# The gradient of z in a linear-attention backward pass: from extra matmul columns to GpSimd and VectorE

## The chip, the cores and the metric

One core of a Trainium2 chip runs the whole kernel. The metric is the device time in microseconds; the kernel before has a median of 641.99 us over six runs (641.56 to 644.08).

## The reference, cut to what matters

The forward pass is a gate over two branches: linear attention with 32 heads of 20 columns, and a two-layer ReLU network. All gradients are asked for as well.

```python
g = _sigmoid((x * gate_w).sum(-1, keepdims=True))
# attention: phi(t) = where(t > 0, t + 1, exp(t)) + 1e-6
pq, pk = phi(q), phi(k)
kv  = einsum("bhsd,bhse->bhde", pk, v)
z   = einsum("bhsd->bhd", pk)                      # sum over the tokens
num = einsum("bhqd,bhde->bhqe", pq, kv)
den = einsum("bhqd,bhd->bhq", pq, z)[..., None] + 1e-6
a   = (num / den) @ wo
b   = relu(x @ w1) @ w2
out = g * a + (1 - g) * b
```

There are 2048 tokens (16 tiles of 128 rows), D = 640 (5 tiles of 128 columns) and 1728 hidden columns. The gradient of z is one number for each of the 640 columns: a sum over all tokens of pq / den times a number for each token and head, with a minus sign. It is wanted in every row of the gradient of k.

## The kernel before

The work is a row of TensorE stages, one after the other: k and the gate, Y = pk^T x, the forward loop over the token tiles (q, the hidden layer, the output), dW2, X, the backward loop over the token tiles (`fb_a` and `fb_b`), dW1, dk, dWk, dWq and dx. A scheduler orders the instructions of every engine by their dependences and their place in the program; each engine then runs its own queue in order. SyncE issues nearly all loads, stores and transposing loads. Large buffers lie in one SBUF tensor, the arena, whose addresses a planner assigns from sizes and rough times of life (`ar.add`, lines 107 to 177), so that buffers of different stages share addresses and a later writer waits for an earlier reader.

The parts that the change and the prediction speak of:

- `pqg(i)` is pq / den times the gate for token tile i (bf16, 128 rows, 640 columns). `doX(i)` holds dO of the tile, loaded by `do_load`, and 32 more columns (`DX = D + H`, line 108). In the forward loop (lines 637 to 655) `do_load` of the next group of four tiles stands at the head of an iteration.
- `r_main(i)`, run for every token tile during the dW2 stage, multiplies dO by M^T, and reduces its product with pqg over each head into `u_all[:, i, :]` (32 columns, f32, line 672). `w32` is `u_all` times `rg_t` (one number for each token, line 674). GpSimd multiplies `zb` by it (line 676), and ScalarE puts it, as bf16, in the 32 extra columns of `doX(i)` (line 677).
- At the end of dW2, GpSimd adds the two halves of its last tile (line 737), after a DMA has moved one half to other partitions. Then VectorE computes `U_t` and `dl_t` (lines 744 to 746).
- X = pqg^T [dO, w32] runs over five tiles of 128 columns of pqg, and for each over the 16 token tiles, as two matmuls of 512 and 160 columns (lines 755 and 756). The first 640 columns are X. Of the last 32, the block diagonal is what is wanted: VectorE multiplies them by the mask `MDh` and sums (line 759) to give -dz, one column of `dz_t`, and spreads it on a diagonal, `dzd` (line 761). In `small_1` a matmul with a matrix of ones sums the rows of `dzd` and so puts dz in all 128 rows (`dzb`).
- `fb_a(i, half)` (lines 766 to 783): ten matmuls of 432 columns fill a PSUM tile, ScalarE scales it into a buffer of the ring `tb` (line 775; eight buffers), VectorE makes a mask from the hidden layer in another one (line 777) and multiplies (line 778); after the second half it copies 64 columns (line 780) and SyncE issues a transposing load. `fb_b` uses that four tiles later.
- `small_0`, after `fb_a` of tile 2, fills five PSUM tiles `dwo`, which ScalarE and VectorE evacuate in turns (lines 344 and 346). `small_1`, after tile 5, starts with a GpSimd memset (line 807), which the scheduler may run as soon as its addresses are free.
- PSUM has four buffers of this size, used in turns by all stages. The SBUF tag `f32` has three.

Of the kernel before, what the change touches and what calls it, by code (L numbers as in the profile page):

```python
# [8 lines left out]
ALU = mybir.AluOpType  # L9
# [71 lines left out]
def kernel(  # L81
# [23 lines left out]
    WMAX = max(hi - lo for lo, hi in WIN)  # L105
    DSPL = [(0, 512), (512, D)]
    DSP1 = [(0, 512), (512, D + 1)]
    DX = D + H
    DQX = D + 16

    ar = _Arena()
# [21 lines left out]
    ar.add("pk", NT * D * B2, 0, T_FF)  # L133
    ar.add("zd", D * B2, 0, T_FF - 5)
    ar.add("YT0", KD * D * B2, T_Y, T_FF + 5)
    ar.add("dzd", D * B2, T_X, T_FB + 50)
    ar.add("warm", 512 * B2, 0, 10)
    ar.add("Y", KD * D * B2, T_Y, T_FF + 20)
    ar.add("KVT", KD * D * B2, 0, T_FF + 30)
# [53 lines left out]
    def aview(name, n_elems, **dims):  # L193
        o = ar.off(name) // 2
        v = arena[:, o:o + n_elems]
        if dims:
            (k, n), = dims.items()
            v = v.rearrange(f"p ({k} z) -> p {k} z", **{k: n})
        return v
# [24 lines left out]
    doTg = [aview(f"doT{g}", G * D, k=KD) for g in range(NG)]  # L224
    hsg = [aview(f"hs{g}", G * FPAD, i=G) for g in range(NG)]
    zd, YT0_s = aview("zd", D), mat("YT0")
    dzd = aview("dzd", D)
    wk_s, wq_s, wv_s, wo_s = aview("wk", KD * DQX, k=KD), mat("wq"), mat("wv"), mat("wo")
    w1_s = aview("w1", KD * F, k=KD)
    w2_s = aview("w2", KF * D, k=KF)  # L230
# [21 lines left out]
    def pqg(i):  # L252
        return pqgg[i // G][:, i % G, :]

    def doX(i):
        return doXg[i // G][:, i % G, :]
# [24 lines left out]
    ones_sq = cpool.tile([P, P], BF16, name="ones_sq")  # L281
    zc_t = cpool.tile([P, KD], FP32, name="zc_t")
    MDw = cpool.tile([P, KD, WMAX], BF16, name="MDw")
    MDh = cpool.tile([P, KD, H], BF16, name="MDh")
    zb = cpool.tile([P, D], BF16, name="zb")
    dzb = cpool.tile([P, D], BF16, name="dzb")
    dz_t = cpool.tile([P, KD], FP32, name="dz_t")
    w1T_tail = cpool.tile([P, D], BF16, name="w1T_tail")
    rg_t = cpool.tile([P, NT], FP32, name="rg_t")
    g_t = cpool.tile([P, NT], FP32, name="g_t")  # L290
# [35 lines left out]
    def after(late, early, wait=False):  # L326
        tc.add_manual_dep(late.ins, early.ins.name, mybir.DependencyInfo(
            mybir.DependencyClass.Sync if wait else mybir.DependencyClass.NoSync,
            mybir.DependencyReason.DATA), reason="order of loads")
# [141 lines left out]
    for i in range(NT):  # L471
        if i >= NPE:
            k_part(i, range(KD))
        if i == 0:
            nc.vector.memset(ones_sq[:], 1.0)
            nc.gpsimd.memset(MDw[:], 1.0)
            nc.gpsimd.memset(MDh[:], 1.0)

    for j in range(KD):
        rel = P * j - WIN[j][0]  # L480
        nc.gpsimd.affine_select(out=MDw[:, j, :], in_=MDw[:, j, :], compare_op=ALU.is_ge, fill=0.0,
                                base=rel, pattern=[[-DH, WMAX // DH], [0, DH]], channel_multiplier=1)
        nc.gpsimd.affine_select(out=MDw[:, j, :], in_=MDw[:, j, :], compare_op=ALU.is_ge, fill=0.0,
                                base=DH - 1 - rel, pattern=[[DH, WMAX // DH], [0, DH]], channel_multiplier=-1)
        nc.gpsimd.affine_select(out=MDh[:, j, :], in_=MDh[:, j, :], compare_op=ALU.is_ge, fill=0.0,
                                base=P * j, pattern=[[-DH, H]], channel_multiplier=1)
        nc.gpsimd.affine_select(out=MDh[:, j, :], in_=MDh[:, j, :], compare_op=ALU.is_ge, fill=0.0,
                                base=DH - 1 - P * j, pattern=[[DH, H]], channel_multiplier=-1)
    nc.gpsimd.memset(KVT_s, 0.0)
    nc.vector.tensor_scalar(rg_t[:], rg_t[:], 1.0, None, ALU.add)  # L490
    nc.vector.reciprocal(g_t[:], rg_t[:])
# [45 lines left out]
    def h_half(i, half):  # L537
        hp = pp("hp")
        for nb in range(2):
            blk = 2 * half + nb  # L540
            for k in range(KD):
                nc.tensor.matmul(hp[:, nb, 0:NBW], lhsT=xT(i, k), rhs=w1_s[:, k, blk * NBW:(blk + 1) * NBW],  # L542
                                 start=(k == 0), stop=(k == KD - 1))
        dst = hs(i)[:, 2 * half * NBW:(2 * half + 2) * NBW].rearrange("p (b c) -> p b c", b=2)
        if half == 0:
            nc.scalar.activation(dst, hp[:, :, 0:NBW], ACT.Relu, scale=omg_t[:, i:i + 1])
        else:
            nc.vector.tensor_scalar(dst, hp[:, :, 0:NBW], omg_t[:, i:i + 1], 0.0, ALU.mult, ALU.max)
            nc.vector.tensor_copy(hs(i)[:, F:FPAD], hs(i)[:, F - FT:F])
            hTs[i] = rnext("hTf").rearrange("p (c s) -> p c s", s=P)  # L550
            hT_ld[0] = load_T(hTs[i], hs(i))
# [8 lines left out]
    def out_chunk(i):  # L560
        pr, ii = i // 2, i % 2
        hT, pqT = hTs.pop(i), pqTs.pop(i)
        if ii == 0:
            ops[i] = pp("op")
        op = ops.pop(i)
        for kf in range(KF - 1):
            mm_cols(op, hT[:, kf, :], lambda a, e: w2_s[:, kf, a:e], ii == 0 and kf == 0, False)
        for k in range(KD):
            mm_cols(op, pqT[:, k, :], lambda a, e: M_s[:, a // P:e // P, k, :], False, ii == 1 and k == KD - 1)
        if ii == 0:  # L570
            ops[i + 1] = pp("op")
            tail_pair(op, ops[i + 1], hT[:, KF - 1, :], hTs[i + 1][:, KF - 1, :], w2_s[:, KF - 1, :], True)
        if ii == 0:
            o_st[pr] = rnext("ost").rearrange("p (i d) -> p i d", i=2)
        nc.scalar.copy(o_st[pr][:, ii, :], flat(op)[:, 0:D])
        jk = tmp("tb", 8)
        nc.vector.scalar_tensor_tensor(jk[:], flat(op)[:, 0:D], 1.0, doX(i)[:, 0:D], ALU.mult, ALU.mult,
                                       accum_out=T_t[:, i:i + 1])
        if ii == 1:
            nc.scalar.dma_start(rows2(o0, pr), o_st.pop(pr))  # L580

    def do_load(g):
        return load_N(doXg[g][:, :, 0:D], do2[g * G * P:(g + 1) * G * P, :])
# [52 lines left out]
    LAG = 2  # L636
    for a in range(2, NT + LAG, 2):
        if a < NT:
            if a % G == 2 and a // G + 1 < NG:
                after(do_load(a // G + 1), M_ld)  # L640
            if a > 2:
                q_main(a)
                q_den(a)
                h_half(a, 0)
            q_post(a)
            h_half(a, 1)
            q_main(a + 1)
            q_den(a + 1)
            h_half(a + 1, 0)
            q_post(a + 1)  # L650
        q_store(a // 2 - 1)
        out_chunk(a - 2)
        if a < NT:
            h_half(a + 1, 1)
        out_chunk(a - 1)
    e_r, dq_st = {}, {}

# [6 lines left out]
    def r_main(i):  # L664
        rp = pp("rp")
        for k in range(KD):
            mm_cols(rp, doTg[i // G][:, k, gsl(i)], lambda a, e: MT_s[:, k, a:e], k == 0, k == KD - 1)
        rb = tmp("tb", 8)
        nc.scalar.copy(rb[:], flat(rp)[:, 0:D])
        t_ = tmp("tb", 8)  # L670
        nc.vector.tensor_tensor(t_[:], rb[:], pqg(i), ALU.mult)
        nc.vector.tensor_reduce(u_all[:, i, :], heads(t_[:]), AX.X, ALU.add)
        w32 = tmp("grd", 3, [P, H], FP32)
        nc.vector.tensor_scalar(w32[:], u_all[:, i, :], rg_t[:, i:i + 1], None, ALU.mult)
        wz = tmp("f32", 3, dt=FP32)
        nc.gpsimd.tensor_tensor(heads(wz[:]), heads(zb[:]), hb(w32[:]), ALU.mult)
        nc.scalar.copy(doX(i)[:, D:DX], w32[:])
        rps[i] = rp, wz

    def r_post(i):  # L680
# [61 lines left out]
                after(ld, last_mm)  # L742
    r_store(NT // 2 - 1)
    nc.vector.tensor_reduce(U_t[:], u_all[:], AX.X, ALU.add)
    nc.vector.tensor_tensor(dl_t[:], g_t[:], T_t[:], ALU.mult)
    nc.vector.tensor_tensor(dl_t[:], U_t[:], dl_t[:], ALU.subtract)

    for q_ in range(2):
        load_T(w1T_s[:, 0:KF - 1, q_ * 320:(q_ + 1) * 320], B_w1[q_ * 320:(q_ + 1) * 320, 0:(KF - 1) * P])
    nc.gpsimd.tensor_copy(w1T_s[:, KF - 1, :], w1T_tail[:, :])  # L750
    for m in range(KD):
        xp = pp("xp")
        for i in range(NT):
            lhsT = pqg(i)[:, csl(m)]
            nc.tensor.matmul(xp[:, 0, :], lhsT=lhsT, rhs=doX(i)[:, 0:512], start=(i == 0), stop=(i == NT - 1))  # L755
            nc.tensor.matmul(xp[:, 1, 0:DX - 512], lhsT=lhsT, rhs=doX(i)[:, 512:DX], start=(i == 0), stop=(i == NT - 1))  # L756
        nc.scalar.copy(X_s[:, m, :], flat(xp)[:, 0:D])
        jz = tmp("grd", 3, [P, H], FP32)
        nc.vector.scalar_tensor_tensor(jz[:], flat(xp)[:, D:DX], -1.0, MDh[:, m, :], ALU.mult, ALU.mult,
                                       accum_out=dz_t[:, m:m + 1])  # L760
        nc.vector.tensor_scalar(dzd[:, csl(m)], ident[:], dz_t[:, m:m + 1], None, ALU.mult)
    load_T(KV2_s, KVT_d)

    dhTs, dx_st = {}, {}
# [41 lines left out]
    def small_1():  # L806
        nc.gpsimd.memset(dKVT_s, 0.0)  # L807
        ps = pp("dzp")
        mm_cols(ps, ones_sq[:], lambda a, e: dzd[:, a:e], True, True)
        nc.scalar.copy(dzb[:], flat(ps)[:, 0:D])  # L810
        blockdiag(dKVT_s, woT_s, XT_s)

# [201 lines left out]
```

## Time and profile before

| What | us |
|---|---|
| median of six runs | 641.99 |
| the profiled execution, its time | 641.73 |
| its span, first to last instruction | 640.0 |
| VectorE busy | 240.8 |
| ScalarE busy | 151.3 |
| GpSimd busy | 98.7 |
| dW2 stage, X stage start | 217.6, 298.2 |
| backward loop start (first `fb_a` matmul) | 321.0 |

The granted TensorE clock is 1.000 in the mean over the span. A row of the order of time has the start and the duration in us, the engine, the line, the operation, output<-inputs, and in brackets the idle time of the engine before it with what ended it. Rows of one operation on a line give the duration in ns as minimum/median/maximum, and then the first and last start. "PE" is TensorE, "DVE" VectorE, "ACT" ScalarE, "POOL" GpSimd, "SP" SyncE.

### The profile page before, as it was taken

How to read it: one execution, taken by the hardware profiler on the slowest of the kernel's cores; microseconds unless marked ns; L12 is line 12 of the kernel's file. 1: busy time of each engine (PE TensorE's matmuls, PEld its weight loads, DVE VectorE, ACT ScalarE, POOL GpSimd, SP SyncE). 2: the span in 40 equal slices, each digit the busy share in tenths (PEclk: the TensorE clock that was granted, in tenths of full speed). 3: DMA queues.
4: the chain of work that ended last, by engine and by line, in shares of the span. 5: the costliest groups of instructions: out<-in, count | busy, mean ns of one | idle time of the engine just before them, and what ended most of it. 6: DMA issues, size and time to landing. Idle time of an engine off the chain costs nothing.

```text
span 640.0 us, 10518 instructions
## 1 busy us (share of the span) xinstructions
PE 635.0 (99%) x4462; PEld 354.5 (55%) x4462; DVE 240.8 (38%) x494; ACT 151.3 (24%) x223; POOL 98.7 (15%) x97
## 2 busy tenths in 40 slices
PE   8999999999999999999999999999999999999998
PEld 4556555555555555555555555555555555555554
DVE  4822754454534146554153332230016320104442
ACT  3512321222211123322153343431100011110000
POOL 5002642454334022322000000000000000000000
PEclk9999999999999999999999999999999999999999
DMA  7998995434355943942869997992228559991111
GB/s 183 344 391 173 254 236 131 120 92 82 87 120 102 268 122 102 193 143 85 188 152 240 256 225 154 195 261 64 89 76 174 139 143 238 244 248 42 42 42 43
DMA packets 227075, 103.69 MB, mean 162 GB/s; under 512 B 183764, under 2 KB 226324, under 8 KB 227028
## 3 DMA queue, kind: packets, MB, share of 16 engines
q1 hardware_dynamic: 216602, 90.23, 61.2%
q10 hardware_dynamic: 10426, 12.78, 5.8%
q8 instruction: 35, 0.57, 0.4%
q14 instruction: 12, 0.10, 0.0%
HBM read 28.43 MB, written 28.84 MB: 89 GB/s over the span
## 4 chain that ended last, share of the span: by engine, by line
PE 98%; ACT 1%; DVE 0%; issue 0%
PE w1p_4596 L857 1%; PE w1p_4727 L857 1%; PE w1p_5115 L857 1%; PE w1p_5047 L857 1%; PE w1p_4824 L857 1%; PE w1p_5240 L857 1%; PE w1p_5183 L857 1%; PE w1p_4978 L857 1%; PE w1p_4659 L857 1%; PE w1p_4528 L857 1%; PE op_2274 L339 1%; PE op_2237 L339 1%; PE op_2137 L339 1%; PE op_1786 L339 1%; PE op_1591 L339 1%; PE op_1554 L339 1%
## 5 line engine op out<-in xcount | busy, mean ns | idle before, releaser
L339 PEld LDWEIGHTS <-arena 128*128 128x128 bf16 x2818 | 218.2, 98 | 169.7 <-DVE arena L346 1.0
L857 PEld LDWEIGHTS <-arena 128*128 128x128 bf16 x320 | 30.8, 98 | 26.9 <-issue 0.5
L771 PEld LDWEIGHTS <-arena 128*128 128x128 bf16 x320 | 30.5, 98 | 26.7 <-issue 1.3
L542 PEld LDWEIGHTS <-arena 128*128 128x128 bf16 x320 | 30.0, 98 | 26.6 <-issue 1.9
L841 DVE TENSOR_TENSOR tb_4802<-dkp_4791,dzb 128x640 bf16<-128x640 f32 x1 | 0.8, 825 | 41.5 <-PE dkp_4791 L339 41.5
L755 PEld LDWEIGHTS <-arena 128*128 128x128 bf16 x80 | 7.8, 98 | 9.5 <-issue 0.3
L944 PEld LDWEIGHTS <-arena 128*128 128x128 bf16 x80 | 7.8, 98 | 9.5
L956 DVE SCALAR_TENSOR_TENSOR f_5645<-gwb,dl_t,arena 128x640 f32<-128x640 bf16 x1 | 0.9, 883 | 26.4 <-DMA arena<-dxB_d 26.4
L361 PEld LDWEIGHTS <-arena 128*128 128x128 bf16 x140 | 7.9, 97 | 1.9 <-issue 0.6
L508 POOL TENSOR_TENSOR f_728<-tb_492,zb 128x640 f32<-128x640 bf16 x1 | 1.4, 1397 | 48.1 <-ACT zb L605 48.1
L756 PEld LDWEIGHTS <-arena 128*128 128x128 bf16 x80 | 7.8, 98 | 0.0
L945 PEld LDWEIGHTS <-arena 128*128 128x128 bf16 x80 | 7.8, 98 | 0.0
L807 POOL MEMSET arena<- 128x3200 bf16 x1 | 2.8, 2764 | 30.5 <-ACT arena L344 30.5
L857 PE MATMUL w1p_4596<-arena 128*128 128x432 bf16 x32 | 6.0, 346 | 0.0
L857 PE MATMUL w1p_4727<-arena 128*128 128x432 bf16 x32 | 6.0, 346 | 0.0
L857 PE MATMUL w1p_4528<-arena 128*128 128x432 bf16 x32 | 6.0, 346 | 0.0
L857 PE MATMUL w1p_4824<-arena 128*128 128x432 bf16 x32 | 6.0, 346 | 0.0
L857 PE MATMUL w1p_5047<-arena 128*128 128x432 bf16 x32 | 6.0, 346 | 0.0
L857 PE MATMUL w1p_5115<-arena 128*128 128x432 bf16 x32 | 6.0, 346 | 0.0
L857 PE MATMUL w1p_4659<-arena 128*128 128x432 bf16 x32 | 6.0, 346 | 0.0
L857 PE MATMUL w1p_4978<-arena 128*128 128x432 bf16 x32 | 6.0, 346 | 0.0
L857 PE MATMUL w1p_5183<-arena 128*128 128x432 bf16 x32 | 6.0, 346 | 0.0
(1048 smaller groups left out, 1189.1 us busy)
## 6 DMA issues: line engine op xcount, KB each, us to landing
out_dram<-arena ACTq DMA_DIRECT2D x28, 160.0 KB, 3.4
arena<-in_A_x_dram SPq DMA_DIRECT2D x6, 640.0 KB, 6.2
pk_d<-arena SPq DMA_DIRECT2D x4, 640.0 KB, 9.4
arena<-in_grad_out_dram SPq DMA_DIRECT2D x4, 640.0 KB, 5.1
e_d<-arena SPq DMA_DIRECT2D x8, 320.0 KB, 2.4
out_dram<-arena ACTq DMA_DIRECT2D x8, 320.0 KB, 2.3
arena<-e_d SPq DMA_DIRECT2D x8, 320.0 KB, 3.8
dq_d<-arena SPq DMA_DIRECT2D x8, 320.0 KB, 4.0
```

Source lines behind the costliest of these rows:

```text
L339: mm = nc.tensor.matmul(ps_tile[:, b, 0:e - a], lhsT=lhsT, rhs=rhs_fn(a, e), start=start, stop=stop, **kw)
L361: nc.tensor.matmul(ps_tile[:, bank, a - 512 * bank:e - 512 * bank], lhsT=lhsT_fn(j), rhs=rhs_mat[:, j, a:e], start=bank not in seen, stop= ...
L508: return nc.gpsimd.tensor_tensor(tzs[i][:], pqs[i][:], zb[:], ALU.mult)
L542: nc.tensor.matmul(hp[:, nb, 0:NBW], lhsT=xT(i, k), rhs=w1_s[:, k, blk * NBW:(blk + 1) * NBW], start=(k == 0), stop=(k == KD - 1))
L755: nc.tensor.matmul(xp[:, 0, :], lhsT=lhsT, rhs=doX(i)[:, 0:512], start=(i == 0), stop=(i == NT - 1))
L756: nc.tensor.matmul(xp[:, 1, 0:DX - 512], lhsT=lhsT, rhs=doX(i)[:, 512:DX], start=(i == 0), stop=(i == NT - 1))
L771: nc.tensor.matmul(gp[:, nb, 0:NBW], lhsT=doTg[i // G][:, k, gsl(i)], rhs=w2T_s[:, k, blk * NBW:(blk + 1) * NBW], start=(k == 0), stop=(k ...
L807: nc.gpsimd.memset(dKVT_s, 0.0)
L857: nc.tensor.matmul(wp[:, nb, 0:NBW], lhsT=xN2[:, i, csl(m)], rhs=hs(i)[:, blk * NBW:(blk + 1) * NBW], start=(i == 0), stop=(i == NT - 1))
L944: nc.tensor.matmul(wp[:, 0, :], lhsT=lhsT, rhs=dqN[:, i, 0:512], start=(i == 0), stop=(i == NT - 1))
L945: nc.tensor.matmul(wp[:, 1, 0:D + 1 - 512], lhsT=lhsT, rhs=dqN[:, i, 512:D + 1], start=(i == 0), stop=(i == NT - 1))
L956: nc.vector.scalar_tensor_tensor(base[:], gwb[:], dl_t[:, i:i + 1], dxB[:, i, :], ALU.mult, ALU.add)
```

## The change

The 32 extra columns of X go, and with them the cast into `doX`, the mask `MDh`, `dz_t` and the diagonal `dzd`. In their place `u_all` is multiplied by `rg_t` once for all tiles. While X runs, GpSimd multiplies `pqg(i)` by `u_all[:, i, :]`, one number for each head of 20 columns, for all 16 token tiles, three or four beside each tile of X, and VectorE adds the 16 products in f32 into `dz_a`, a buffer of the tag `f32`. A last VectorE operation changes the sign and makes bf16 of it, `dzs`: 128 rows of partial sums. The matmul with ones in `small_1`, which sums rows anyway, takes `dzs` in place of the diagonal. The arena's `doX` buffers get smaller, which gives the planner other addresses. Besides, `do_load` of the next group moves to the end of the iteration, between `h_half(a + 1, 1)` and `out_chunk(a - 1)`.

```diff
-    DX = D + H
+    DX = D
...
-    ar.add("dzd", D * B2, T_X, T_FB + 50)
+    ar.add("dzs", D * B2, T_X, T_FB + 50)
...
-    MDh = cpool.tile([P, KD, H], BF16, name="MDh")
...
-            nc.gpsimd.memset(MDh[:], 1.0)
...
-        nc.gpsimd.affine_select(out=MDh[:, j, :], in_=MDh[:, j, :], compare_op=ALU.is_ge, fill=0.0,
-                                base=P * j, pattern=[[-DH, H]], channel_multiplier=1)
...
     for a in range(2, NT + LAG, 2):
         if a < NT:
-            if a % G == 2 and a // G + 1 < NG:
-                after(do_load(a // G + 1), M_ld)
...
             h_half(a + 1, 1)
+            if a % G == 2 and a // G + 1 < NG:
+                after(do_load(a // G + 1), M_ld)
         out_chunk(a - 1)
...
         nc.gpsimd.tensor_tensor(heads(wz[:]), heads(zb[:]), hb(w32[:]), ALU.mult)
-        nc.scalar.copy(doX(i)[:, D:DX], w32[:])
...
     nc.vector.tensor_reduce(U_t[:], u_all[:], AX.X, ALU.add)
+    nc.vector.tensor_tensor(u_all[:], u_all[:], rg_t[:].unsqueeze(2).to_broadcast([P, NT, H]), ALU.mult)
...
+    dz_a = tmp("f32", 3, dt=FP32)
     for m in range(KD):
         xp = pp("xp")
         for i in range(NT):
-            lhsT = pqg(i)[:, csl(m)]
-            nc.tensor.matmul(xp[:, 0, :], lhsT=lhsT, rhs=doX(i)[:, 0:512], start=(i == 0), stop=(i == NT - 1))
-            nc.tensor.matmul(xp[:, 1, 0:DX - 512], lhsT=lhsT, rhs=doX(i)[:, 512:DX], start=(i == 0), stop=(i == NT - 1))
+            mm_cols(xp, pqg(i)[:, csl(m)], lambda a, e: doX(i)[:, a:e], i == 0, i == NT - 1)
         nc.scalar.copy(X_s[:, m, :], flat(xp)[:, 0:D])
-        jz = tmp("grd", 3, [P, H], FP32)
-        nc.vector.scalar_tensor_tensor(jz[:], flat(xp)[:, D:DX], -1.0, MDh[:, m, :], ALU.mult, ALU.mult,
-                                       accum_out=dz_t[:, m:m + 1])
-        nc.vector.tensor_scalar(dzd[:, csl(m)], ident[:], dz_t[:, m:m + 1], None, ALU.mult)
+        for i in range(NT * m // KD, NT * (m + 1) // KD):
+            pr_ = dz_a if i == 0 else tmp("f32", 3, dt=FP32)
+            nc.gpsimd.tensor_tensor(heads(pr_[:]), heads(pqg(i)), hb(u_all[:, i, :]), ALU.mult)
+            if i > 0:
+                nc.vector.tensor_tensor(dz_a[:], dz_a[:], pr_[:], ALU.add)
+    nc.vector.tensor_scalar(dzs[:], dz_a[:], -1.0, None, ALU.mult)
...
-        mm_cols(ps, ones_sq[:], lambda a, e: dzd[:, a:e], True, True)
+        mm_cols(ps, ones_sq[:], lambda a, e: dzs[:, a:e], True, True)
```

`mm_cols` issues one matmul for each of the column ranges 0 to 512 and 512 to 640.

More of the change, by code (lines that the diff above doesn't have):

```diff
@@ L226 @@
     zd, YT0_s = aview("zd", D), mat("YT0")
-    dzd = aview("dzd", D)
+    dzs = aview("dzs", D)
     wk_s, wq_s, wv_s, wo_s = aview("wk", KD * DQX, k=KD), mat("wq"), mat("wv"), mat("wo")
@@ L283 @@
     MDw = cpool.tile([P, KD, WMAX], BF16, name="MDw")
-    MDh = cpool.tile([P, KD, H], BF16, name="MDh")
     zb = cpool.tile([P, D], BF16, name="zb")
     dzb = cpool.tile([P, D], BF16, name="dzb")
-    dz_t = cpool.tile([P, KD], FP32, name="dz_t")
     w1T_tail = cpool.tile([P, D], BF16, name="w1T_tail")
@@ L484 @@
                                 base=DH - 1 - rel, pattern=[[DH, WMAX // DH], [0, DH]], channel_multiplier=-1)
-        nc.gpsimd.affine_select(out=MDh[:, j, :], in_=MDh[:, j, :], compare_op=ALU.is_ge, fill=0.0,
-                                base=P * j, pattern=[[-DH, H]], channel_multiplier=1)
-        nc.gpsimd.affine_select(out=MDh[:, j, :], in_=MDh[:, j, :], compare_op=ALU.is_ge, fill=0.0,
-                                base=DH - 1 - P * j, pattern=[[DH, H]], channel_multiplier=-1)
     nc.gpsimd.memset(KVT_s, 0.0)
```

## The prediction

> **What bounds the kernel now.** I read the page's first part and its chain of waits, then the waits of TensorE, then the rows of the X stage, then the order of time on VectorE, GpSimd and TensorE around it (296 to 345 us).
>
> ```profile
> PE 635.0 (99%) x4462; PEld 354.5 (55%) x4462; DVE 240.8 (38%) x494; ACT 151.3 (24%) x223; POOL 98.7 (15%) x97
> PE 98%; ACT 1%; DVE 0%; issue 0%
> ...
> PE warm_129 L430 <- DVE arena L386: 1.3, 1, 1.3
> PE kp_161 L339 <- ACT arena L344: 0.5, 1, 0.5
> PE kp_228 L339 <- DVE arena L383: 0.2, 1, 0.2
> ```
>
> TensorE is busy for 635.0 of 640.0 us, the chain that ends last is 98% TensorE, and its only waits over 0.15 us add up to 2.0 us, all in the first stage. So a column less in a matmul is time gained, and any new wait of TensorE is time lost: there is no slack in which to catch up. VectorE (38%) and GpSimd (15%) have room on the average, which says nothing about one stage.
>
> ```profile
> L756 PE MATMUL xp_3232<-arena x16: 232/233/233, 298.4 to 302.7; 128*128 128x160 bf16 x16
> L756 PE MATMUL xp_3269<-arena x16: 232/233/233, 303.0 to 307.3; 128*128 128x160 bf16 x16
> ...
> 532.53 4.35 PE wkp_5325 L339 x32
> 536.88 4.35 PE wkp_5360 L339 x32
> ```
>
> The first two rows: the five X tiles start 4.56 us apart (298.44 to 303.00), 16 pairs of 512 and 160 columns each, so 285 ns a pair. The last two, from the chain of waits in order of time: a tile of 16 pairs of 512 and 128 columns, the size that X gets, takes 4.35 us, 272 ns a pair.
>
> ```profile
> L745 DVE TENSOR_TENSOR dl_t<-g_t,T_t x1: 176/176/176, 219.4 to 219.4; 128x16 f32<-128x16 f32 x1
> ...
> 296.89 0.82 DVE L746 TENSOR_TENSOR dl_t<-U_t,dl_t 128x16 f32<-128x16 f32 x1
> ...
> 296.41 1.27 POOL L676 TENSOR_TENSOR f_3152<-zb,grd_3150 128x640 f32<-128x640 bf16 x1 [3.35 <-DVE grd_3150 L674]
> 302.39 1.53 POOL L737 TENSOR_TENSOR arena<-f_3219,f_3220 64x640 bf16<-64x640 f32 x1 [4.71 <-DMA f_3220<-f_3219]
> ...
> 334.14 0.81 DVE L346 CAST arena<-dwo_3553 128x640 bf16<-128x640 f32 x1
> 334.88 2.34 DVE L780 COPY arena<-arena 128x64 bf16<-128x64 bf16 x1
> 334.96 2.48 DVE L777 TENSOR_SCALAR tb_3584<-arena 128x864 bf16<-128x864 bf16 x1
> ```
>
> These decide the forecast. L745 and L746 are the same VectorE operation on the same shape, two SBUF inputs of 16 columns. The first takes 176 ns, the second 823, and it ends at 297.71, just when GpSimd's L676 ends (296.41 + 1.27 = 297.68): it stood still while GpSimd worked. Likewise L780, 181 ns in the median, takes 2.34 us beside GpSimd's memset L807 (334.42 to 337.18).
>
> **What the skill says, and whether the trace agrees.** "SBUF — State Buffer", section "SBUF: two separate sides": VectorE and GpSimd arbitrate for one pair of SBUF ports; a VectorE operation in a two-port mode, or with two SBUF inputs against a GpSimd operation that reads SBUF, and a GpSimd operation exclude each other, and "the other fully blocks". L746 and L780 agree. "VectorE: DVE Perf Modes", section "Why `tensor_tensor` can't do 2×_2P or 4×": such an operation in fp32 has no fast mode; the f32 reduction L744 (512 columns, 0.68 us) fits one element a cycle. "TensorE: Matmul & The Clock Gate", section "What's actually happening": after an idle window of about 3.4 us the clock is halved, until about 3.4 us of work have passed. Before shows it only at the start: five 512-column matmuls of L430 take 2.31 us, where X does a 512 and a 160 together in 285 ns.
>
> **The change, part by part.** I sum against the profiled execution (641.73 us, span 640.0, so 1.7 us outside it); the median of the six runs is 641.99.
>
> 1. X loses 32 columns in 80 matmuls: 5 x (4.56 - 4.35) = 1.05 us off TensorE, on the path. The order of instructions on TensorE is otherwise the same.
>
> 2. Removed beside the path: 16 casts L677 (0.22 us each), five times L759 and L761 (0.19 + 0.08 + 0.25 us), eleven small GpSimd operations on MDh before 57 us, when GpSimd then idles (48.1 us before L508). Nothing on TensorE waits for any of them: 0.
>
> 3. The moved load of dO and the smaller arena. do_load(1) is issued at 74.04 us now, is 640 KB and lands in about 5 us; its first reader (L577 of chunk 4) comes after 114 us. Passing a few stores and transposes on SP costs it about 10 us of some 35. The new addresses also change which loads wait for which readers; on SP the two pqg loads now go ahead of the first doT transpose (issued at 205.51), whose first user, r_main(0), starts at 224.11: some 10 us spare. Later queue swaps are alike. I take 0, bounds -0.3 to +1.
>
> 4. Added: GpSimd multiplies pqg(i) by u_all, 16 times, f32 out from bf16 and a broadcast f32, the form of L676: 1.27 us each. VectorE adds 15 of them into dz_a: f32, two SBUF inputs; nearest rows L684 and L841, 0.82 us. Then dzs, a two-port copy, about 0.45. Where do they run? Product 0 goes ahead of the dW2 tail add L737, which waits for its DMA until 302.39; the other 15 stand behind it, from 302.39 + 1.53 = 303.9. If the two engines overlapped, GpSimd would set the pace: 15 x 1.27. But each add excludes each product. Bounds of a step: 1.27 (full overlap) and 2.2 (1.27 + 0.82 + 0.1 of handover). L676-like operations back to back start 1.22 apart (L522 to L527, 92.53 and 93.75), and VectorE's 0.82 us rows follow 0.73 apart at best: 1.95. I take 2.0. The chain ends at D = 303.9 + 15 x 2.0 + 0.5 = 334.4. The three f32 buffers, one held by dz_a, only make product n+2 wait for add n.
>
> 5. Who waits for D? dzs itself is wanted late (small_1, after fb_a(5)). But all adds and dzs stand in VectorE's in-order queue ahead of the first mask of fb_a, which runs at 322.35 now. TensorE can finish six halves of fb_a and two tiles of small_0 (four PSUM buffers hold the last four), until about 332.7 - 1.05 = 331.6. ScalarE's fifth evacuation needs a tb buffer (eight, two for each half) that VectorE's first multiply L778 frees. So small_0 stops, then limps. Then fb_a(3, 0), which starts at 334.14 now, needs the PSUM buffer of the second small_0 tile, which VectorE's cast L346 frees, and that stands behind five halves and a mask: a half is 0.38 + 0.11 (L777 to L778, 337.44 to 337.55) + 0.53 (to the next) = 1.02; 5 x 1.02 + two copies L780 at 0.2 + 0.38 + 0.82 = 6.7 us. In between, the memset L807 comes due when small_0's last matmul ends, about D + 4.4, and holds copies and masks up as in the rows above: at most 2.76, taken at 2.5. So fb_a(3, 0) starts at D + 9.2 = 343.6, 9.5 us late. The gain of step 1 is inside this: PE arrives 1.05 earlier and waits longer.
>
> 6. Both stalls of TensorE are some 5 us (331.6 to D + 2.2, and D + 4.4 to D + 9.2). By the clock page it then runs at half speed for about 3.4 us, 1.7 lost; bounds 0 and 3.7 (two windows); I take 2.0.
>
> Sum: 641.73 + 9.5 + 2.0 + 0 = 653.2. The median stands 0.26 above the profiled execution; I say 653.3. After fb_a(3, 0) I see no further loss: the first dhT transpose is ready around D + 6.5 and wanted at D + 16.5.
>
> **The rivals.** Not slower (ends on the other side): adds and products overlap, because the lock is held for only a part of an operation. With a step of 1.27, D = 303.9 + 19.1 + 0.5 = 323.5; the first L778 is at 324.06 now, and the delay is absorbed by buffers. Time 641.99 - 1.05 = 640.9. It decides below a step of about 1.5 us: D must be under 326 or so, that is 333.1 (the start of fb_a(3, 0) less the gain) - 6.7. For it: GpSimd's rows beside VectorE grow only a little (L508: 1.40 alone, 1.47 beside L526). Against it: L746.
>
> Half way: steps of 1.6 to 1.8 us, and a memset that finds a gap, no clock loss: D = 330 at 1.7 us, fb_a(3, 0) at 336.7, 2.6 us late: 641.99 + 2.6 = 644.6.
>
> Worse: steps of 2.3 us (products slower than L676, each handover dear), D = 338.9, 348.1 for fb_a(3, 0), and 3.7 for the clock: 641.73 + 14 + 3.7 = 659.4.
>
> **How the numbers follow.** Main case 0.68, half way 0.10, worse 0.11, not slower 0.11. The main case alone spans about 648 to 657 (a step of 1.85 to 2.15, the clock 0 to 3.7). 644 to 659 leaves out the not-slower case, some 0.04 of half way and 0.05 of worse: 0.20. What can be told from no change is 0.2%, 1.28 us; the not-slower case lies at 1.05, so of its 0.11 I give 0.07 to no change and 0.04 to faster; 0.89 to slower.
>
> **What would show it.** X tiles 4.35 us apart; the adds on VectorE starting about 2 us apart and ending near the end of a product; dzs near 334; TensorE waits of some 5 us before the third small_0 tile (on ScalarE) and before fb_a(3, 0) (on VectorE), then matmuls at half speed. It is wrong if the adds take 0.8 us beside running products, or if TensorE shows a new wait elsewhere, on a DMA.

## The result, and the profile after

The kernel after takes 661.36 us in the median (659.76 to 664.27, ten runs), against 642.01 for the kernel before beside it (641.56 to 644.08, twenty runs): 1.0304 times as long, 95% interval 1.0292 to 1.0316. The profiled execution took 659.34 us, with a span of 657.6 against 640.0. The direction was as predicted, and so was the mechanism that the prediction describes; but the time lies beyond the range of 644 to 659, for a second cause that it had put at nothing.

First the page: busy time of each engine, and the share of each in the chain that ended last.

```profile
PE 639.7 (97%) x4462; PEld 356.0 (54%) x4462; DVE 266.9 (41%) x496; ACT 148.2 (23%) x207; POOL 117.4 (18%) x102
PE 89%; DVE 6%; DMA 3%; issue 1%; ACT 1%; POOL 0%; DVEq 0%; ACTq 0%
```

TensorE was 98% of the chain; now VectorE has 6% of it and DMA 3%. TensorE's waits (what it waited for: total us, times, longest) name three places:

```profile
PE dwo_3549 L359 <- ACT tb_3507 L769: 5.7, 1, 5.7
PE gp_3576 L765 <- DVE arena L344: 3.9, 1, 3.9
PE rp_2370 L337 <- DMA arena<-in_grad_out_dram: 3.1, 1, 3.1
```

The first two are the ones that the prediction names (the third `small_0` tile on ScalarE, `fb_a(3, 0)` on VectorE's cast). The third is not in it: the first matmul of `r_main(0)`, some 76 us before the X stage, waits for the transposing load of dO.

The X stage itself, in the order of time of each engine (start, duration in us; in brackets the idle time before and what ended it):

```profile
316.79 4.51 PE L337 MATMUL xp_3332<-arena 128*128 128x512 bf16 x32
321.14 4.51 PE L337 MATMUL xp_3375<-arena 128*128 128x512 bf16 x32
...
331.39 1.27 POOL L752 TENSOR_TENSOR f_3409<-arena,u_all 128x640 f32<-128x640 bf16 x1 [0.76 <-DVE f_3204 L754]
333.42 1.27 POOL L752 TENSOR_TENSOR f_3412<-arena,u_all 128x640 f32<-128x640 bf16 x1 [0.76 <-DVE f_3204 L754]
...
331.41 1.92 DVE L754 TENSOR_TENSOR f_3204<-f_3204,f_3372 128x640 f32<-128x640 f32 x1
333.44 1.93 DVE L754 TENSOR_TENSOR f_3204<-f_3204,f_3409 128x640 f32<-128x640 f32 x1
...
339.53 0.82 DVE L754 TENSOR_TENSOR f_3204<-f_3204,f_3418 128x640 f32<-128x640 f32 x1
340.39 0.49 DVE L755 TENSOR_SCALAR arena<-f_3204 128x640 bf16<-128x640 f32 x1
```

X tiles start 4.35 us apart, the gain of 0.21 a tile. Products and adds start 2.03 us apart, and an add that starts 0.02 us after a product takes 1.92 us; the last one, with no product beside it, takes 0.82. The chain ends at 340.39 + 0.49 = 340.88.

Between that and `fb_a(3, 0)`, on GpSimd and VectorE:

```profile
345.52 2.80 POOL L801 MEMSET arena<- 128x3200 bf16 x1 [6.78 <-PE dwo_3567 L359]
...
345.25 0.38 DVE L771 TENSOR_SCALAR tb_3509<-arena 128x864 bf16<-128x864 bf16 x1
346.25 2.31 DVE L771 TENSOR_SCALAR tb_3526<-arena 128x864 bf16<-128x864 bf16 x1
348.48 0.81 DVE L344 CAST arena<-dwo_3540 128x640 bf16<-128x640 f32 x1
```

A mask takes 2.31 us in place of 0.38 beside the memset, and the cast that frees the PSUM buffer comes only then. The clock, from a table of stretches (us; busy time of PE, PEld, DVE, ACT, POOL with instructions; granted clock; DMA share; GB/s):

```profile
335.00:340.60 5.60, 2.31 (x23) 1.51 (x22) 5.25 (x5) 0.00 (x0) 2.54 (x2) 1.00 0.00 0
340.60:344.00 3.40, 0.80 (x7) 0.64 (x7) 3.05 (x8) 1.99 (x3) 0.00 (x0) 0.50 0.00 0
344.00:347.40 3.40, 1.44 (x14) 1.27 (x14) 3.16 (x7) 1.83 (x3) 1.88 (x1) 0.50 0.97 181
347.40:350.80 3.40, 1.46 (x5) 0.61 (x5) 3.40 (x6) 0.00 (x0) 0.92 (x1) 0.50 0.97 170
350.80:354.30 3.50, 3.50 (x11) 1.41 (x10) 0.27 (x2) 0.98 (x1) 0.00 (x0) 0.50 1.29 200
354.30:357.70 3.40, 3.40 (x20) 1.86 (x19) 1.79 (x5) 1.25 (x2) 0.00 (x0) 1.00 1.03 319
```

Half speed lasts for four of these stretches, 13.65 us by the clock's records, and ends after the one in which TensorE is busy throughout. What it costs is half of the time in which matmuls run in it without a stop: from 349.34, where `fb_a(3, 0)` starts, to 354.3, that is 5 us at half speed, 2.5 lost.

Now the third wait. The chain that ended last, in order of time, passes through it:

```profile
213.29 5.00 PE op_2261 L337 x36
218.28 2.77 PE w2p_2318 L337 x21
221.05 6.85 DMA arena<-in_grad_out_dram
227.90 0.05 issue
227.95 2.84 PE rp_2370 L337 x10
```

The load lands at 227.90. Without it TensorE would have gone on at about 224.8 (227.95 less the wait of 3.1), and the ten matmuls of `rp_2370` then run at half speed too: 2.84 us where the same group takes 1.52 in the full-speed kernels below. SP's queue after, and then before, shows why the load is late:

```profile
206.05 1.84 SPq L330 DMA_DIRECT2D arena<-pqg_d  x2
207.99 5.73 SPq L322 DMA_TRANSPOSE arena<-in_grad_out_dram  x1
213.81 0.53 SPq L330 DMA_DIRECT2D arena<-e_d  x1
214.40 5.29 SPq L322 DMA_TRANSPOSE arena<-in_grad_out_dram  x1
219.77 1.18 SPq L330 DMA_DIRECT2D arena<-e_d  x2
221.05 6.89 SPq L322 DMA_TRANSPOSE arena<-in_grad_out_dram  x2
```

```profile
205.51 4.24 SPq L324 DMA_TRANSPOSE arena<-in_grad_out_dram  x1
209.81 0.57 SPq L332 DMA_DIRECT2D arena<-pqg_d  x1
```

A transposing load of dO holds SP for 3.0 to 7.7 us while it is issued (all four of each kernel), and rows follow one another without a gap, so the place in the queue is the time. Before, the load that `r_main(0)` needs is the first transposing load; after, it is the third. By the addresses that the planner gives out, the first at 207.99 is the one for token rows 1024 to 1535, which is needed much later. The planner puts the first group's dO^T on the addresses of `pqT`, which the last matmuls of the forward loop read (`op_2261`, until 218.3); in the kernel before it lay on those of `xT3` and `w1`, which are free earlier. So the scheduler puts the load behind `op_2261`, and in SP's queue it comes behind the transposing load of 214.40 too.

Where the 17.6 us of the span went, by the starts of the stages, after less before: 0.49 at the start of the Y stage; 0.53 at dW2; 5.5 at X (303.74 against 298.22), so 5.0 in dW2 (3.1 of waiting, 1.7 of half clock, some 0.2 unexplained); 15.2 at `fb_a(3, 0)` (349.34 against 334.14), so 9.7 more in X and `small_0`; 17.6 at the third half of `fb_a` from there, `fb_a(4, 0)` (355.41 against 337.79), so 2.4 for the clock. Behind that nothing is added.

### The profile page after: what moved, and what is told of

It is laid out like the page before. It is cut to its first block, busy times and chain, and to the rows that moved or that the text cites. A ratio compares the mean times of both kernels' runs of the same rounds, so it can differ in the third digit from the quotient of the medians.

```text
span 657.6 us, 10536 instructions
## 1 busy us (share of the span) xinstructions
PE 639.7 (97%) x4462; PEld 356.0 (54%) x4462; DVE 266.9 (41%) x496; ACT 148.2 (23%) x207; POOL 117.4 (18%) x102
## 4 chain that ended last, share of the span: by engine, by line
PE 89%; DVE 6%; DMA 3%; issue 1%; ACT 1%; POOL 0%; DVEq 0%; ACTq 0%
DVE f_3204 L754 4%; DMA arena<-arena 1%; DMA arena<-in_grad_out_dram 1%; PE w1p_4732 L851 1%; PE w1p_4601 L851 1%; PE w1p_4664 L851 1%; PE w1p_5245 L851 1%; PE w1p_5188 L851 1%; PE w1p_5120 L851 1%; PE w1p_5052 L851 1%; PE w1p_4983 L851 1%; PE w1p_4829 L851 1%; PE w1p_4533 L851 1%; PE op_2261 L337 1%; PE op_2224 L337 1%; PE op_2124 L337 1%
## 5 line engine op out<-in xcount | busy, mean ns | idle before, releaser
L950 DVE SCALAR_TENSOR_TENSOR f_5650<-gwb,dl_t,arena 128x640 f32<-128x640 bf16 x1 | 0.9, 884 | 23.8 <-DMA arena<-dxB_d 23.8
L765 PE MATMUL gp_3576<-arena 128*128 128x432 bf16 x10 | 3.8, 559 | 3.9 <-DVE arena L344 3.9
L851 PE MATMUL w1p_4601<-arena 128*128 128x432 bf16 x32 | 6.0, 346 | 0.0
L851 PE MATMUL w1p_4732<-arena 128*128 128x432 bf16 x32 | 6.0, 346 | 0.0
L851 PE MATMUL w1p_4664<-arena 128*128 128x432 bf16 x32 | 6.0, 346 | 0.0
L851 PE MATMUL w1p_4829<-arena 128*128 128x432 bf16 x32 | 6.0, 346 | 0.0
L851 PE MATMUL w1p_5052<-arena 128*128 128x432 bf16 x32 | 6.0, 346 | 0.0
L851 PE MATMUL w1p_4533<-arena 128*128 128x432 bf16 x32 | 6.0, 346 | 0.0
L851 PE MATMUL w1p_4983<-arena 128*128 128x432 bf16 x32 | 6.0, 346 | 0.0
L851 PE MATMUL w1p_5120<-arena 128*128 128x432 bf16 x32 | 6.0, 346 | 0.0
L851 PE MATMUL w1p_5188<-arena 128*128 128x432 bf16 x32 | 6.0, 346 | 0.0
```

Source lines behind the costliest of these rows:

```text
L765: nc.tensor.matmul(gp[:, nb, 0:NBW], lhsT=doTg[i // G][:, k, gsl(i)], rhs=w2T_s[:, k, blk * NBW:(blk + 1) * NBW], start=(k == 0), stop=(k ...
L851: nc.tensor.matmul(wp[:, nb, 0:NBW], lhsT=xN2[:, i, csl(m)], rhs=hs(i)[:, blk * NBW:(blk + 1) * NBW], start=(i == 0), stop=(i == NT - 1))
L950: nc.vector.scalar_tensor_tensor(base[:], gwb[:], dl_t[:, i:i + 1], dxB[:, i, :], ALU.mult, ALU.add)
```

## The experiments

The theory: the time has two separate causes. The first is the chain of products and adds, with the stalls behind it and the clock: about 11.5 us. The second is the arena's new addresses: 5 us in the profiled execution. The rivals: that the arena wait comes from the moved `do_load`; that products or adds alone are too slow for the X stage; and that the chain's length lies in the buffers, not in the shared ports. Each ratio below is to the kernel before, run beside it, with its 95% interval. From the products without adds on, every kernel has the old addresses (the 32 unused columns), except the one called the new addresses alone.

**The addresses as before.** `doX` keeps its 32 columns, unused, so that the arena's sizes and addresses are those of before; all else is the kernel after.

```diff
-    DX = D
+    DX = D + H
```

> The changed kernel with doX buffers of the old size (DX = D + 32, the 32 columns unused), so that the arena has its old addresses; all else as changed, the moved load too. Theory (two causes: the new addresses make the first doT transpose late, and the products and adds exclude each other): no wait before r_main(0); the adds still 2.03 us apart, dzs near 335.5, fb_a(3, 0) near 344, clock halved once for some 14 us; 654.5 us. Rival (the moved load of dO makes doT late): TensorE still waits 3 us before r_main(0), about 661 us.

653.40 us (652.92 to 653.75), ratio 1.0175 (1.016 to 1.019). TensorE's waits:

```profile
PE dwo L359 <- ACT tb L769: 5.3, 2, 5.1
PE gp L765 <- DVE arena L344: 3.9, 1, 3.9
```

The wait on the DMA is gone, the other two stay. So 8.0 us of the median (661.36 - 653.40) hang on 32 columns of a buffer that nobody reads. What remains is the predicted mechanism alone, and its time is the forecast of 653.3 (closer than the terms of the sum, as the account below shows).

**The small `doX`, one load earlier.** The lifetime of the first dO^T buffer begins 20 units of the planner's time earlier, so that it gets an address that is free sooner; the columns stay off. The planner lays out the rest anew as well (the other three dO^T buffers move too), so this is not the kernel after with one address changed.

```diff
-        ar.add(f"doT{g}", G * P * KD * B2, T_DW2 + 10 + 6 * g, T_FB + 12 + 30 * (g + 1))
+        ar.add(f"doT{g}", G * P * KD * B2, T_DW2 + 10 + 6 * g - 20 * (g == 0), T_FB + 12 + 30 * (g + 1))
```

> The changed kernel, with the small doX, but the planner is told that doT0 lives from 20 us earlier, so that it may not share addresses with what the last forward tiles read. Theory: the first doT transpose is issued before 210 and TensorE does not wait before r_main(0); 654.5 us, the same as with the old sizes. Rival (the denser arena costs by other loads as well): 1 us or more above the kernel with old sizes.

654.25 us (653.64 to 654.31), ratio 1.0187 (1.0172 to 1.0202). The queue of SP has the load first again, and TensorE doesn't wait for it:

```profile
205.38 4.41 SPq L322 DMA_TRANSPOSE arena<-in_grad_out_dram  x1
209.84 0.57 SPq L330 DMA_DIRECT2D arena<-pqg_d  x1
```

So the size of `doX` as such does not bring the wait: with the load early again it is gone, though other addresses moved in the same edit. That the smaller buffers by themselves cost nothing is seen to within the 0.9 us between this kernel and the last.

**The moved load alone**, in the kernel before:

```diff
         if a < NT:
-            if a % G == 2 and a // G + 1 < NG:
-                after(do_load(a // G + 1), M_ld)
...
             h_half(a + 1, 1)
+            if a % G == 2 and a // G + 1 < NG:
+                after(do_load(a // G + 1), M_ld)
```

> The kernel before with one edit of the change alone: do_load of the next group at the end of the iteration. Theory (it has some 30 us to spare): no new wait of TensorE, 642.0 us, within 0.2%. Rival (later traffic of dO pushes the transposes of the forward loop): a wait in the forward loop or before r_main(0), 644 us or more.

642.15 us, ratio 0.9998 (0.999 to 1.0006), and no new wait behind the first stage. The rival that blames this move alone falls. (The new addresses with the load in its old place were not run.)

**Products without adds**, on the old addresses:

```diff
-            if i > 0:
-                nc.vector.tensor_tensor(dz_a[:], dz_a[:], pr_[:], ALU.add)
```

> Old doX sizes, and the 15 adds left out (dz then holds the product of token tile 0 alone); the 16 GpSimd products stay. Theory (each engine alone fits beside X): products 1.27 us apart or less, done near 322, first mask of fb_a near 321.5, no new wait of TensorE; 641.99 - 1.05 = 640.9 us. Rival (GpSimd's products alone hold up VectorE's masks by the ports): 645 us or more.

640.87 us (640.5 to 642.9), ratio 0.9982 (0.9975 to 0.9989). GpSimd's last rows of the stage:

```profile
306.84 14.77 POOL L752 TENSOR_TENSOR f<-arena,u_all 128x640 f32<-128x640 bf16 x12
```

Twelve products in 14.77 us, 1.23 each, done at 321.6: GpSimd alone fits into the X stage.

**Adds without products** (two products are kept, to have something to add), again on the old addresses:

```diff
-            pr_ = dz_a if i == 0 else tmp("f32", 3, dt=FP32)
-            nc.gpsimd.tensor_tensor(heads(pr_[:]), heads(pqg(i)), hb(u_all[:, i, :]), ALU.mult)
+            if i < 2:
+                pr_ = dz_a if i == 0 else tmp("f32", 3, dt=FP32)
+                nc.gpsimd.tensor_tensor(heads(pr_[:]), heads(pqg(i)), hb(u_all[:, i, :]), ALU.mult)
```

> Old doX sizes, and only the products of token tiles 0 and 1 (the 15 adds all stay and add tile 1's product 15 times). Theory: with GpSimd quiet an add takes 0.8 us and follows 0.75 to 0.85 us after the one before it; dzs near 317, no new wait of TensorE; 640.9 us. Rival (a chain of dependent f32 adds takes about 1.9 us a step by itself): adds 1.9 us apart, dzs near 334, 650 us or more.

641.14 us, ratio 0.9987 (0.998 to 0.9995).

```profile
305.23 12.86 DVE L755 TENSOR_TENSOR f<-f,f 128x640 f32<-128x640 f32 x15 [5.54 <-POOL f L753]
```

Fifteen adds in 12.86 us, 0.86 each. So either half alone costs nothing and takes no wait; both together take 2.03 us a step, hardly less than the sum, 1.23 + 0.86 = 2.09.

**More buffers.** Is it the ports that keep the two apart, or that product n + 2 must wait for add n to give its buffer back? Five buffers in place of three, at all places of the tag (two of the places are shown):

```diff
-    dz_a = tmp("f32", 3, dt=FP32)
+    dz_a = tmp("f32", 5, dt=FP32)
...
-            pr_ = dz_a if i == 0 else tmp("f32", 3, dt=FP32)
+            pr_ = dz_a if i == 0 else tmp("f32", 5, dt=FP32)
```

> The changed kernel with old doX sizes and five f32 buffers in place of three, so that four products can be under way. Theory (product and add exclude each other at the ports, whatever the buffers): four products go ahead of the dW2 tail add and the chain starts earlier, but a step stays at 1.95 to 2.05 us; dzs about 2 us earlier than with three buffers, near 333; 651.3 us. Rival (the two engines are coupled by the two free buffers alone): products 1.22 us apart beside adds of 0.82 us, dzs near 322, no new wait of TensorE, 640.9 us.

652.18 us (650.6 to 654.44), ratio 1.0147 (1.0132 to 1.0163), and in the orders of time of the two engines:

```profile
308.87 20.91 DVE L754 TENSOR_TENSOR f<-f,f 128x640 f32<-128x640 f32 x12 [1.16 <-POOL f L752]
...
306.99 21.18 POOL L752 TENSOR_TENSOR f<-arena,u_all 128x640 f32<-128x640 bf16 x12
```

The last add, with no product beside it, takes 0.83 us, so a step is (20.91 - 0.83) / 11 = 1.83 us; without the first step it is 1.81, from the add at 310.85 to the one at 327.14. That lies between the two answers. The products no longer wait for buffers and yet come 1.81 apart in the same stretch, not 1.23, so the larger part is the engines' hold on each other; but 2.03 - 1.81 = 0.2 us of a step was the buffers', and the two overlap by 2.09 - 1.81 = 0.3 us when a product is always ready. The chain ends at 330.3, 5 us earlier than with three buffers, and the kernel gains only 1.2, for two reasons that TensorE's waits show:

```profile
PE gp L765 <- DVE arena L344: 5.0, 1, 5.0
PE dxp L337 <- DVE gcol L943: 2.8, 1, 2.8
```

The memset now falls at 334.65 to 337.46, where a mask that takes 3.03 us stands ahead of the same cast. And five buffers let the dx stage's operation L950 run ahead into the dWq stage. There it waits for a load of its own input, with four casts behind it in VectorE's queue that free PSUM buffers:

```profile
581.37 0.89 DVE L950 SCALAR_TENSOR_TENSOR f<-gwb,dl_t,arena 128x640 f32<-128x640 bf16 x1 [18.30 <-DMA arena<-dxB_d]
582.17 0.35 DVE L943 CAST gcol<-wqp 128x1 bf16<-128x1 f32 x4
```

With three buffers these casts run one by one from 572.92 on. The profiled execution is the slowest of the four (654.44); two others (650.6 and 651.49) have a granted clock of 0.995 in place of 0.992, so not every run need have this second wait.

**The memset out of the way.** Its share of the second stall, on the old addresses: it waits for ScalarE's evacuation of `fb_a(4, 0)`.

```diff
-        nc.scalar.activation(gs[:], gp[:, :, 0:NBW], ACT.Copy, scale=omg_t[:, i:i + 1])
+        fb_act[i, half] = nc.scalar.activation(gs[:], gp[:, :, 0:NBW], ACT.Copy, scale=omg_t[:, i:i + 1])
...
-        nc.gpsimd.memset(dKVT_s, 0.0)
+        after(nc.gpsimd.memset(dKVT_s, 0.0), fb_act[4, 0], wait=True)
```

> The changed kernel with old doX sizes, and the memset of dKVT made to wait for ScalarE's evacuation of fb_a(4, 0), so that it comes after the second stall. Theory (the memset holds VectorE's masks for 2.2 us before the cast that TensorE waits for): the wait before fb_a(3, 0) falls from 3.9 to about 1.7 us; 651.2 us, or 650.5 if the clock then recovers earlier. Rival (the wait is that of the queued masks and multiplies alone): 653.4 us as before.

651.45 us, ratio 1.0145 (1.0131 to 1.0159), 1.95 less than with the memset in its place.

```profile
PE gp L765 <- DVE arena L344: 2.0, 1, 2.0
```

The wait is 3.9 - 2.0 = 1.9 us shorter, which is what the mask lost (2.32 - 0.38 with the memset beside it). So the memset has its share, 1.9 us where 2.5 was forecast.

**Both parts on VectorE.** The other way to part the two engines: the products go to VectorE as well, GpSimd does nothing for dz.

```diff
-            nc.gpsimd.tensor_tensor(heads(pr_[:]), heads(pqg(i)), hb(u_all[:, i, :]), ALU.mult)
+            nc.vector.tensor_tensor(heads(pr_[:]), heads(pqg(i)), hb(u_all[:, i, :]), ALU.mult)
```

> The changed kernel with old doX sizes, and the 16 products made by VectorE too; GpSimd does nothing for dz. Theory (31 VectorE operations of about 0.85 us with no engine to exclude them, from 299 on, are shorter than 15 steps of 2.03 us from 304 on): dzs near 325.5, fb_a's buffers absorb the rest, no wait of TensorE over 0.5 us; 641.0 us. Rival (VectorE doing all is the longer chain): dzs after 330, 645 us or more.

641.50 us (640.89 to 641.83), ratio 0.9989 (0.9982 to 0.9995). One engine does product and add in 1.53 us, less than two engines together (2.03, or 1.81 with five buffers). The second product still waits until 304.12 for a buffer that GpSimd's dW2 tail add holds, and dz is done at 328.4; TensorE then waits 0.2 us for the cast.

**The new addresses alone.** Products on VectorE as in the last kernel, the arena as after (the moved load stays in):

```diff
-    DX = D + H
+    DX = D
```

> After as it is (DX = D, so the arena's new addresses), but the 16 products on VectorE, so that GpSimd and VectorE do not shut each other out during X. If the late transposing load of dO of token rows 0 is a cost of its own that the arena's new addresses bring, TensorE waits some 3 us for it (rp matmul on a DMA from in_grad_out), and runs at half clock for one record of about 3.4 us: 641.5 (v1_dve, with the old addresses) + 3.1 + 1.7 = 646.3; range 645 to 648. If that wait only came up together with the stalls behind the adds, or is hidden without them, the time is that of v1_dve, 641 to 642.5.

649.36 us (648.91 to 650.33), ratio 1.0112 (1.0097 to 1.0127).

```profile
PE rp L337 <- DMA arena<-in_grad_out_dram: 4.8, 1, 4.8
...
PE gp L765 <- DVE arena L344: 0.9, 1, 0.9
```

The late load is a cost of its own, with no stall behind adds beside it. The amount expected was 3 us short: in this execution the load landed later (its SP row with the one behind it takes 7.93 us, 6.89 in the profile of after), and half speed lasted two stretches, not one:

```profile
224.00:227.30 3.30, 0.47 (x4) 0.14 (x2) 0.00 (x0) 0.00 (x0) 0.00 (x0) 1.00 1.05 210
227.30:230.70 3.40, 1.40 (x5) 0.64 (x6) 0.00 (x0) 0.00 (x0) 0.00 (x0) 0.50 1.13 263
230.70:234.10 3.40, 3.40 (x15) 1.65 (x14) 1.15 (x2) 0.69 (x1) 0.00 (x0) 0.50 0.01 2
```

TensorE starts again at 229.3, so 4.8 us at half speed: 2.4 lost. With the 4.8 of waiting and 0.7 more on the cast that is 7.9, as measured (649.36 - 641.50 = 7.86). It is also what the medians gave between after and the old addresses, 8.0. The profiled execution of after, 659.34, is shorter than all of its ten timed runs, so the 5.0 us that it shows in dW2 is probably a cheap case of this wait. The granted clocks point the same way: the profile of after and four of its timed runs have 0.987, five stretches of half speed in 657.6 us; the other six have 0.982 to 0.985, six or seven stretches, and are longer (medians 660.5 and 662.2). All five runs of the kernel here have 0.994 or 0.995, two stretches.

**A version that beats before and after.** Products on VectorE, in two buffers of their own, with the old addresses (the edit is to the kernel with both parts on VectorE):

```diff
-            pr_ = dz_a if i == 0 else tmp("f32", 3, dt=FP32)
+            pr_ = dz_a if i == 0 else tmp("pr", 2, dt=FP32)
```

> v1_dve, with the products in two buffers of their own (a new tag) in place of the tag f32, so that the second product needn't wait for the dW2 tail add on GpSimd (until 304.1 in v1_dve). The chain of products and adds, 16 x 0.8 + 15 x 0.83 = 25 us from about 299, then ends near 324.5 in place of 327.9. If the 0.2 us wait on VectorE and the missing 0.4 us of gain in v1_dve came from VectorE ending late, the time is 640.9, that of b1_no_add (the floor for 32 columns less in X). If what v1_dve lacks is scatter or elsewhere, 641.5, as v1_dve.

641.17 us (640.52 to 641.5), ratio 0.9983 (0.9974 to 0.9992). VectorE and TensorE in order of time:

```profile
324.08 0.83 DVE L754 TENSOR_TENSOR f<-f,pr 128x640 f32<-128x640 f32 x1
324.94 0.49 DVE L755 TENSOR_SCALAR arena<-f 128x640 bf16<-128x640 f32 x1
...
331.23 2.33 PE L359 MATMUL dwo<-arena 128*128 128x140 bf16 x35
333.39 2.90 PE L765 MATMUL gp<-arena 128*128 128x432 bf16 x15
```

dz is done at 325.4, all five tiles of `small_0` run without a stop (35 matmuls in 2.33 us), and `fb_a(3, 0)` follows at once. The gain over before, 0.17%, is that of the kernel with no adds at all (0.9982): what 32 columns less in X are worth. From the kernel with both parts on VectorE (0.9989, 0.9982 to 0.9995) the intervals do not set it apart.

## Why the prediction was wrong in its amount, step by step

1. X: right. Tiles 4.35 us apart; a kernel in which nothing else got in the way has a ratio of 0.9982, 1.2 us, against 1.05.

2. The removed work beside the path: right, no kernel here shows a change that would need it.

3. The moved load and the smaller arena: this is the step that failed. Its first half holds (the moved load alone: ratio 0.9998). Its second half took "the first doT transpose (issued at 205.51), whose first user, r_main(0), starts at 224.11: some 10 us spare" and put the new addresses at 0, at most 1. The first doT transpose in the new queue was not the same load: it was that of another group of tokens, and the one that `r_main(0)` uses had become the third, issued at 221.05 in place of 205.51. The step took transposes of one kind for one another, without following which rows of dO each one loads. It costs 5.0 us in the profiled execution and 7.9 to 8.0 in the medians (a load that lands 3 to 5 us late, and half speed after it). The 653.3 of the forecast lacks just this term: without it the kernel takes 653.40.

4. The chain: right in kind and size. The step is 2.03, predicted 2.0. On the old addresses the chain ends at 335.35, predicted 334.4; of the difference, 15 x 0.03 = 0.45 is the step, and the rest a later start. The two engines exclude each other in the main, as the Trainium skill says ("SBUF — State Buffer", section "SBUF: two separate sides"): alone, products take 1.23 and adds 0.86, together 2.03. That the place is a pair of ports is the skill's statement; the traces show only the exclusion. But "the other fully blocks" is more than the run with five buffers shows, where 0.3 of 2.09 us overlaps. And I wrote that the three buffers "only" make a product wait for an add; that was 0.2 us of a step.

5. The stalls: right. On the old addresses `fb_a(3, 0)` starts at 343.82, predicted 343.6. Inside it the memset was put 0.6 too high (2.5 for 1.9) and the chain's end 0.95 too early, which nearly cancel; that much of the agreement is luck. That the adds block VectorE's queue, and not that dz is late, is seen in the same trace: the matmul with ones that takes `dzs` starts at 364.69, 29 us after dz is done at 335.35. (The kernels without adds or without products can't tell the two apart, since their dz is early as well.)

6. The clock: predicted 2.0, measured 2.4 in after (17.6 - 15.2) and 2.3 on the old addresses (span 652.0, less 640.0, less 9.7 at `fb_a(3, 0)`). I took 3.4 us of work at half speed to be the rule; in fact the stretch in which work starts again counts as well. The sum's last step is off by 0.2: 653.2 and the 0.26 of the median make 653.5, not 653.3.

Of the rivals, "not slower" fell with the step of 2.03. "Half way" has its chain in the kernel with five buffers (a step of 1.8, the end at 330.3 for 330), but not its price: the memset finds no gap there, and `fb_a(3, 0)` starts at 339.49, not at 336.7. "Worse" is near the measured time, 659.4, by coincidence: neither its step of 2.3 nor its end of the chain at 338.9 is what happened. The prediction's last sentence, "a new wait elsewhere, on a DMA", names the way in which it failed, but step 3 gave it at most 1 us.

What stays open: how long the timed runs of after wait for the load (only one execution of it was profiled; the clocks say that six of the ten ran at half speed for one or two stretches more, not in which stall), whether the new addresses cost the same with the load of dO in its old place, and whether the version that wins could give the 32 columns back, with the lifetime of the first dO^T buffer moved; that was not run.

## What to carry to other kernels

Work that is given to "idle" engines beside a stage must be priced on both engines at once, and its end compared with what stands behind it in the in-order queue, not with the time at which its result is wanted: here VectorE alone did both parts in 1.53 us a step, where two engines took 2.03. When a buffer in a planned arena changes its size, follow every load by the rows it loads, to its new place in the queue and to its first reader: "the first transpose" before and after need not be the same one.

## What the runs showed of the hardware that was not expected

- Half speed comes in stretches of 3.41 us: the clock's records show 3.41 (the late load in after), 6.83 (five buffers), 10.24 (memset moved) and 13.65 us (after). It ended each time only after a stretch in which TensorE was busy throughout; stretches with 0.80, 1.44 and 1.46 us of work in them, as in the table above, stayed slow, and so did two with 2.2 and 2.3 us in the kernel with the memset moved (337.23 to 344.05). It begins more easily: a stretch that still had 1.2 us of work in it was followed by half speed (580.16 to 583.57 with five buffers), one with 1.9 was not (330.40 to 333.81 with the memset moved). So the window before it need not be idle throughout, as the prediction has it from the skill. The Trainium skill has the window, free-running, and its length ("TensorE: Matmul & The Clock Gate", section "What's actually happening"), and the runs agree. What follows for a price: the loss is half of the time from the restart to the end of the first fully busy stretch. Here it was 1.7 (restart 227.95, end 231.4), 2.4 (229.3 to 234.1), 2.5 (349.34 to 354.3) and 2.8 (341.79 to 347.47, memset moved). By the place of the restart it would lie between 1.7 and 3.4 us, half of one and of two stretches; the upper end is an estimate that no run reached.
- With the memset moved away, `fb_a(3, 0)` started 2.0 us earlier (341.79 against 343.82) but the span fell by only 1.6 (652.0 to 650.4): the earlier restart fell nearer to the start of a stretch and ran longer at half speed.
